# Pooled attention and a SiLU layer: selection matmuls in full 128-row shapes, and key transposition as a matmul with the identity

## The chip, the cores and the metric

The kernel runs on one core of a Trainium2 chip. The metric is the device time of one execution in microseconds, as the median of several runs. A core has engines that run side by side and wait for each other by semaphores: TensorE (PE; its weight loads are shown apart as PEld), VectorE (DVE), ScalarE (ACT), GpSimd (POOL) and SyncE (SP), the last two here mainly as issuers of transfers. A matmul takes a weight tile, of so many rows (the dimension summed over, laid out over SBUF partitions) by so many columns (the rows of the result), and moves columns of a second operand through it; the result goes to PSUM.

## The reference

Eight batches, eight heads, 576 positions, 64 elements per head. Keys and values are pooled over groups of eight positions, so each head has 72 pooled keys; then plain softmax attention, and a layer with SiLU on the result (4608 tokens, 512 to 2048 to 512).

```python
def _attn_ref(q, k, v):
    B, H, S, D = q.shape              # 8, 8, 576, 64
    pool = 8
    Sp = S // pool                    # 72
    scale = 1.0 / np.sqrt(D)
    k_p = k.reshape(B, H, Sp, pool, D).mean(axis=3)
    v_p = v.reshape(B, H, Sp, pool, D).mean(axis=3)
    scores = scale * np.matmul(q, k_p.transpose(0, 1, 3, 2))
    # ... softmax over the last axis ...
    return np.matmul(attn, v_p)

def _moe_ref(x, w_in, w_out):
    h = x @ w_in
    g = h * (1.0 / (1.0 + np.exp(-h)))
    return g @ w_out
```

## The kernel before

The kernel works on tiles of 512 tokens. While TensorE computes the layer of one tile (`up`, then `down`), the attention of the next batch is woven into its stream at fixed places. The layer's products are computed in part by a scheme with seven products of quarters instead of eight, which is where VectorE gets much of its work. The stream starts with products of zeros (`warm_up`) while the first data is on its way.

Pooling differs by batch. For batches 0 to 2, the 576 pooled rows of all heads (8 heads of 72) are laid out over 128 partitions in five slots: four slots of 128 rows and a last one of 64. A head of 72 rows therefore lies across slots. Matmuls with pieces of an identity matrix ("selection") bring each head's rows to their place: for the keys with the sums as weights, which also transposes them (32 weight columns at a time), for the values with a shifted identity as weights.

```python
shifts = singles.tile([128, SP + 128 + SP], BF16, name="shifts")   # SP = 72
ident = shifts[:, SP : SP + 128]           # zeros, identity, zeros
# ...
RE = POOL * D
ROWS = H * SP                              # 576
SLOTS = ROWS // 128                        # 4
REST = ROWS - 128 * SLOTS                  # 64
k5, v5 = (singles.tile([128, SLOTS + 1, D], BF16, name=f"{n}5") for n in "kv")
# ...
def segments(h):
    r = SP * h
    while r < SP * (h + 1):
        i = r // 128
        e = min(SP * (h + 1), 128 * (i + 1))
        yield i, (128 if i < SLOTS else REST), r - 128 * i, r - SP * h, e - r
        r = e

def select_k(b, a):
    st = batches[b]
    if a == 0:
        st["kz_ps"] = ps_tile([128, 2, 2, SP], FP32, "at", "kz_ps")
    for c in range(2):
        for s in range(4):
            for i, n, r, sp, m in segments(4 * a + s):
                nc.tensor.matmul(
                    st["kz_ps"][32 * s : 32 * (s + 1), a, c, sp : sp + m],
                    lhsT=k5[:n, i, c * DH : (c + 1) * DH],
                    rhs=ident[:n, r : r + m], start=True, stop=True,
                )
# ...
def select_v(b, a, tag="at"):
    # ...
    for h in range(4 * a, 4 * (a + 1)):
        segs = list(segments(h))
        for j, (i, n, r, sp, m) in enumerate(segs):
            x = SP + r - sp
            nc.tensor.matmul(
                st["v_ps"][:SP, h, :], lhsT=shifts[:n, x : x + SP], rhs=v5[:n, i],
                start=(j == 0), stop=(j == len(segs) - 1),
            )
```

Each of `select_k` and `select_v` is called twice per batch, for heads 0 to 3 and 4 to 7. Rows 64 to 127 of the last slot's inputs are set to zero once at the start, so the sums there are zero.

For batches 3 to 7 each head's 72 pooled rows lie on 72 partitions, and the keys are transposed by TensorE:

```python
def k_transpose(b, parts=(0, 1)):
    st = batches[b]
    kT_ps = ps_tile([128, 2, 2, SP], BF16, "at", "kT_ps")
    for a in parts:
        for c in range(2):
            nc.tensor.transpose(
                kT_ps[:, a, c, :],
                st["kp"][:, a, c].rearrange("k s d -> k (s d)"),
                ident[:SP, :SP],
            )
    a0, a1 = parts[0], parts[-1] + 1
    nc.scalar.copy(kz[b % 2][:, a0:a1], kT_ps[:, a0:a1])
```

The start of the stream, where batch 0 is worked on (cut):

```python
warm_up(19)
slot_sums("k", 0)
select_k(0, 0)
copy_k(0, 0, act_copy)
warm_up(4)
q_transpose(0, 0, 0)
scores(0, part(0, 0))
slot_sums("k", 1)
warm_up(3)
select_k(0, 1)
copy_k(0, 1, act_copy)
# ...
slot_sums("v", 1)
warm_up(1)
numerators(0, part(0, 0), ("mm", "at"))
warm_up(2)
select_v(0, 1, "mm")
copy_v(0, 1)
q_transpose(0, 1, 1)
# ...
```

Of the kernel before, what the change touches and what calls it, by code (L numbers as in the profile page):

```python
# [27 lines left out]
FP32 = mybir.dt.float32  # L28
FP32R = mybir.dt.float32r
BF16 = mybir.dt.bfloat16  # L30
# [6 lines left out]
def kernel(  # L37
# [9 lines left out]
    nc = tc.nc  # L47
# [3 lines left out]
    SP = S // POOL  # L51
# [17 lines left out]
    DH = D // 2  # L69
# [12 lines left out]
    singles = ctx.enter_context(tc.tile_pool(name="singles", bufs=1))  # L82
    big = ctx.enter_context(tc.tile_pool(name="big", bufs=1))
    mid = ctx.enter_context(tc.tile_pool(name="mid", bufs=2))
# [6 lines left out]
    def ps_tile(shape, dtype, tag, name):  # L91
        return psum.tile(shape, dtype, tag=tag, bufs=banks[tag], name=name)

    shifts = singles.tile([128, SP + 128 + SP], BF16, name="shifts")
    ident = shifts[:, SP : SP + 128]
    ones = singles.tile([SP, 32], BF16, name="ones")
    warm = singles.tile([128, 512], BF16, name="warm")
# [17 lines left out]


    kz = [singles.tile([128, 2, 2, SP], BF16, name=f"kz{n}") for n in range(2)]
    gate = singles.tile([128, 1], FP32, name="gate")  # L120

    batches = {}

# [63 lines left out]
    def add_halves(raw):  # L187
        nc.vector.tensor_add(
            out=raw[:, :, : 2 * D], in0=raw[:, :, : 2 * D], in1=raw[:, :, 2 * D :]
        )  # L190

    def add_rest(dst, raw):
        nc.vector.tensor_add(
            out=dst,
            in0=raw[:, :, :D].rearrange("k h (c d) -> k h c d", c=2),
            in1=raw[:, :, D : 2 * D].rearrange("k h (c d) -> k h c d", c=2),
        )

    def pool_k(b, stage):
        st = batches[b]  # L200
        raw = st["k_raw"]
        if stage == 0:
            add_halves(raw)
            return
        st["kp"] = mid.tile([SP, 2, 2, 4, DH], BF16, tag="kp", bufs=1, name="kp")
        for i in range(2):
            add_rest(
                st["kp"][:, i].rearrange("k c s d -> k s c d"), raw[:, 4 * i : 4 * (i + 1)]
            )

    def pool_v(b):
# [4 lines left out]

    def k_transpose(b, parts=(0, 1)):
        st = batches[b]
        kT_ps = ps_tile([128, 2, 2, SP], BF16, "at", "kT_ps")
        for a in parts:  # L220
            for c in range(2):
                nc.tensor.transpose(
                    kT_ps[:, a, c, :],
                    st["kp"][:, a, c].rearrange("k s d -> k (s d)"),
                    ident[:SP, :SP],
                )
        a0, a1 = parts[0], parts[-1] + 1
        nc.scalar.copy(kz[b % 2][:, a0:a1], kT_ps[:, a0:a1])
# [5 lines left out]
    SLOTS = ROWS // 128  # L234
    REST = ROWS - 128 * SLOTS
    k5, v5 = (singles.tile([128, SLOTS + 1, D], BF16, name=f"{n}5") for n in "kv")
# [44 lines left out]
    def segments(h):  # L281
        r = SP * h
        while r < SP * (h + 1):
            i = r // 128
            e = min(SP * (h + 1), 128 * (i + 1))
            yield i, (128 if i < SLOTS else REST), r - 128 * i, r - SP * h, e - r
            r = e

    def select_k(b, a):
        st = batches[b]  # L290
        if a == 0:
            st["kz_ps"] = ps_tile([128, 2, 2, SP], FP32, "at", "kz_ps")
        for c in range(2):
            for s in range(4):
                for i, n, r, sp, m in segments(4 * a + s):
                    nc.tensor.matmul(  # L296
                        st["kz_ps"][32 * s : 32 * (s + 1), a, c, sp : sp + m],
                        lhsT=k5[:n, i, c * DH : (c + 1) * DH],
                        rhs=ident[:n, r : r + m], start=True, stop=True,
                    )  # L300

    def copy_k(b, a, copy=nc.vector.tensor_copy):
# [2 lines left out]
# [3 lines that stand above are left out]
            st["v_ps"] = ps_tile([128, H, D], FP32, tag, "v_ps")  # L308
            st["vp"] = mid.tile([SP, H, D], BF16, tag="vp", name="vp")
        for h in range(4 * a, 4 * (a + 1)):  # L310
            segs = list(segments(h))
            for j, (i, n, r, sp, m) in enumerate(segs):
                x = SP + r - sp
                nc.tensor.matmul(
                    st["v_ps"][:SP, h, :], lhsT=shifts[:n, x : x + SP], rhs=v5[:n, i],
                    start=(j == 0), stop=(j == len(segs) - 1),
                )

# [397 lines left out]
    attn_tables()  # L716
    nc.vector.memset(warm, 0.0)
    nc.vector.memset(ones, float(POOL))
    nc.gpsimd.memset(shifts, 0.0)
    make_identity(nc, ident, nomemset=True)  # L720

# [17 lines left out]
# [11 lines that stand above are left out]
    q_transpose(0, 1, 0)  # L750
# [3 lines left out]
    slot_sums("v", 0)  # L754
    warm_up(2)
    select_v(0, 0, "mm")
    copy_v(0, 0, act_copy)
    denominators(0, part(1, 0))
# [4 lines left out]
# [5 lines that stand above are left out]
# [21 lines left out]
    for t in range(NT):  # L789
        a = t + 1  # L790
# [41 lines left out]
        if a < B:  # L832
            q_at = [15, 16, 17, 8] if t > 1 else [24, 25, 26, 2] if t else [82, 84, 86, 88]
            if t == 0:
                for j in range(2):
                    f_up.append((44 + 8 * j, lambda j=j: slot_sums("k", j)))
                    f_up.append((72 + 8 * j, lambda j=j: select_k(1, j)))
                    f_up.append((72 + 8 * j, lambda j=j: copy_k(1, j)))
                    f_down.append((20 + 10 * j, lambda j=j: slot_sums("v", j)))
                    f_down.append((37 + 3 * j, lambda j=j: select_v(1, j, "at")))  # L840
                    f_down.append((37 + 3 * j, lambda j=j: copy_v(1, j)))
            elif t == 1:
                for j in range(2):
                    f_up.append((0, lambda j=j: slot_sums("k", j, halves=True)))
                    f_up.append((22, lambda j=j: select_k(2, j)))
                    f_up.append((23, lambda j=j: copy_k(2, j)))
                    f_down.append((8, lambda j=j: slot_sums("v", j, halves=True)))
                    f_down.append((40, lambda j=j: select_v(2, j, "at")))
                    f_down.append((41, lambda j=j: copy_v(2, j)))
            else:  # L850
                f_up.append((22, lambda: k_transpose(a)))
                f_down.append((10, lambda: pool_v(a)))
# [3 lines left out]
            if t == 0:  # L856
                f_down.append((0, lambda: load_half_2("k", 0)))
                f_down.append((0, lambda: load_q(2)))
                f_down.append((0, lambda: load_half_2("k", 1)))
                for half in range(2):  # L860
                    f_down.append((31, lambda half=half: load_half_2("v", half)))
                for y in range(2):
                    for n in U_W:
                        f_down.append((6, lambda y=y, n=n: unit_weight_sum(y, n)))
            elif a + 1 < B:
                for stage in range(2):
                    f_down.append((100, lambda stage=stage: pool_k(a + 1, stage)))
                f_up.append((0, lambda: load_one(a + 1, "k")))
                f_up.append((48 if a + 1 == B - 1 else 1, lambda: load_q(a + 1)))
                f_up.append((2, lambda: load_rest(a + 1, "k")))  # L870
                f_down.append((11, lambda: load_one(a + 1, "v")))
                f_down.append((12, lambda: load_rest(a + 1, "v")))
# [49 lines left out]
```

The softmax here doesn't subtract the row's maximum and nothing guards it: scores larger than these inputs give would overflow.

## Time and profile before

| what | value |
|---|---|
| time, median of 3 runs | 286.77 us (286.44 to 287.31) |
| span of the profiled execution | 284.8 us |
| granted TensorE clock | full |
| key selections (line 296) | 72 matmuls: 66 of 128 rows, 6 of 64 rows, 32 weight columns |
| value selections (line 314) | 36 matmuls: 33 of 128 rows, 3 of 64 rows, 72 weight columns |
| key transpositions (line 222) | 20, of 72 rows, 128 weight columns |
| median length of one | 190, 199 and 195 ns |
| ScalarE copy after a transposition (line 228) | 5, of 417 ns |

In the profile's rows a matmul is written as line, tiles (out<-in), weight rows*columns, and rows x columns of the moving operand. Matmuls are pipelined and their ends are modelled, so lengths overlap; the distance from one start to the next tells more. A row's idle time stands in square brackets with what ended it.

### The profile page before, as it was taken

To read this page: it belongs to the slowest core of one execution; us is meant where nothing else is said; L and a number is where in the kernel's file an instruction comes from. 1 tells how busy PE (TensorE), PEld (TensorE's weight loads), DVE (VectorE), ACT (ScalarE), POOL (GpSimd) and SP (SyncE) were. 2 spreads that over 40 slices of the span, in tenths; PEclk is the share of its full clock that TensorE was granted. 3 is DMA by queue.
4 is the path that set the end of the run, shared out by engine and by line. 5 is a ranking of instruction groups with operands and counts; after the bars stand their busy time and mean duration, and the time that the engine had idled before them with its cause. 6 is when DMAs were issued, how large, how long until landed. Compare 5 with 4: busy or idle time off the path is not lost.

```text
span 284.8 us, 6920 instructions
## 1 busy us (share of the span) xinstructions
PE 278.0 (98%) x2773; PEld 196.0 (69%) x2793; DVE 225.1 (79%) x403; ACT 183.8 (65%) x359; POOL 52.2 (18%) x68
## 2 busy tenths in 40 slices
PE   8989999999999999999999999999999999999995
PEld 3348544465777677767888886677677867787684
DVE  4887854979969796979698969986998686836773
ACT  1577676458656886688568857794779558325700
POOL 8664317402030011101200101054100000000000
PEclk9999999999999999999999999999999999999999
DMA  7999999793849565964895396839970032005004
GB/s 211 277 266 227 219 306 183 214 199 70 153 69 210 124 96 95 145 148 126 140 177 156 72 147 113 176 59 170 150 142 0 2 85 65 2 9 139 1 3 147
DMA packets 35296, 37.70 MB, mean 132 GB/s; under 512 B 9952, under 2 KB 27616, under 8 KB 35264
## 3 DMA queue, kind: packets, MB, share of 16 engines
q0 software_dynamic: 21760, 20.86, 43.0%
q1 hardware_dynamic: 12928, 15.48, 22.2%
q10 hardware_dynamic: 576, 0.92, 0.9%
q8 instruction: 22, 0.36, 0.6%
q14 instruction: 10, 0.08, 0.1%
HBM read 36.70 MB, written 9.44 MB: 162 GB/s over the span
## 4 chain that ended last, share of the span: by engine, by line
PE 94%; DVE 3%; ACT 1%; issue 1%; DVEq 0%
PE hp_ps L547 25%; PE o_psP L655 15%; PE o_psQ L655 15%; PE u_psQ L488 7%; PE u_psP L488 7%; PE o_psR L655 5%; PE sc_ps L351 4%; PE warm_ps L704 4%; PE o_ps L582 3%; PE nu_ps L395 3%; PE u_psR L488 2%; PE den_ps L369 2%; DVE w_sum L633 1%; PE kz_ps L296 1%; DVE xT L404 1%
## 5 line engine op out<-in xcount | busy, mean ns | idle before, releaser
L547 PE MATMUL hp_ps<-xT,w_in_sb 128*128 128x512 bf16 (+3 forms) x397 | 80.8, 338 | 1.4 <-ACT h_T L553 0.4
L655 PEld LDWEIGHTS <-h_sum 128*128 128x128 bf16 x640 | 60.6, 98 | 11.9 <-issue 1.3
L553 ACT ACTIVATE h_T<-hp_ps 128x512 bf16<-128x512 f32 (+2 forms) x95 | 51.4, 546 | 26.3 <-PE hp_ps L547 24.9
L547 PEld LDWEIGHTS <-w_in_sb 128*128 128x128 bf16 x412 | 39.3, 98 | 25.0 <-issue 1.4
L615 DVE TENSOR_TENSOR h_sum<-h_T 128x1024 bf16<-128x1024 bf16 (+1 forms) x72 | 50.8, 743 | 7.0 <-ACT h_T L553 7.0
L359 ACT ACTIVATE es<-sc_ps 72x384 bf16<-72x384 f32 (+1 forms) x100 | 39.0, 470 | 10.0 <-PE sc_ps L351 9.9
L488 PEld LDWEIGHTS <-w_sum 128*128 128x128 bf16 x300 | 29.4, 98 | 7.7
L655 PEld LDWEIGHTS <-h_T 128*128 128x128 bf16 x256 | 24.1, 98 | 4.4 <-issue 0.9
L404 DVE TENSOR_TENSOR xT<-nu_ps,rec 128x384 bf16<-128x384 f32 (+1 forms) x50 | 24.0, 532 | 0.3
L378 ACT ACTIVATE lnd<-den_ps 128x384 f32<-128x384 f32 (+1 forms) x23 | 11.1, 484 | 20.2 <-PE den_ps L369 20.2
L153 DVE STREAM_TRANSPOSE qT<-q_bf 128x576 bf16<-128x576 bf16 x32 | 23.0, 753 | 0.0
L182 POOL DMA_DIRECT2D raw<-in_k_dram x5 | 7.0, 1398 | 79.2 <-DVE h_sum L615 28.8
L496 ACT ACTIVATE h_T<-c_sb 128x512 bf16<-128x512 f32 x30 | 18.1, 625 | 5.0 <-DVE c_sb L520 5.0
L274 DVE TENSOR_TENSOR raw<-raw 128x384 f32<-128x384 f32 (+3 forms) x20 | 12.4, 618 | 7.5 <-DMA raw<-in_v_dram 4.3
L655 PE MATMUL o_psP<-w_out_sb,h_sum 128*128 128x256 bf16 x128 | 17.6, 273 | 0.0
L655 PE MATMUL o_psQ<-w_sum,h_sum 128*128 128x256 bf16 x128 | 16.7, 273 | 0.0
L655 PE MATMUL o_psQ<-w_out_sb,h_sum 128*128 128x256 bf16 x128 | 16.6, 273 | 0.0
L655 PE MATMUL o_psQ<-w_sum,h_T 128*128 128x256 bf16 x128 | 16.5, 273 | 0.0
L655 PE MATMUL o_psP<-w_sum,h_T 128*128 128x256 bf16 x128 | 16.5, 273 | 0.0
L520 DVE TENSOR_TENSOR c_sb<-u_psP,t_sb 128x512 f32<-128x512 f32 x15 | 10.2, 678 | 7.1 <-PE u_psP L488 3.6
L655 PE MATMUL o_psR<-w_sum,h_sum 128*128 128x256 bf16 x128 | 15.7, 273 | 0.0
L655 PE MATMUL o_psP<-w_sum,h_sum 128*128 128x256 bf16 x128 | 15.4, 272 | 0.0
(77 smaller groups left out, 417.1 us busy)
## 6 DMA issues: line engine op xcount, KB each, us to landing
out_dram<-o_sb SPq DMA_DIRECT2D x128, 64.0 KB, 3.0
q_bf<-in_q_dram POOLq DMA_DIRECT2D x6, 576.0 KB, 11.1
raw<-in_k_dram SPq DMA_DIRECT2D x6, 512.0 KB, 5.0
raw<-in_k_dram POOLq DMA_DIRECT2D x5, 576.0 KB, 9.1
raw<-in_v_dram POOLq DMA_DIRECT2D x5, 576.0 KB, 8.6
raw<-in_v_dram SPq DMA_DIRECT2D x5, 512.0 KB, 7.6
w_in_sb<-in_moe_w_in_dram POOLq DMA_DIRECT2D x8, 256.0 KB, 8.4
w_out_sb<-in_moe_w_out_dram POOLq DMA_DIRECT2D x4, 512.0 KB, 13.5
```

Source lines behind the costliest of these rows:

```text
L153: nc.vector.transpose(out=st["qT"][:, a, f * QF : (f + 1) * QF].rearrange("r i c p -> r (i c p)"), in_=st["q_bf"][:, a, f * n : (f + 1) * n],)
L274: nc.vector.tensor_add(out=raw[..., :w], in0=raw[..., :w], in1=raw[..., w : 2 * w])
L351: nc.tensor.matmul(sc[s][:, cs], lhsT=kz[b % 2][rows, g, c, :], rhs=st["qT"][rows, g, i0:i1, c, :], start=(c == 0), stop=(c == 1),)
L359: nc.scalar.activation(es[:, s, :], sc[s], func=AF.Exp, scale=score_scale)
L404: nc.vector.tensor_mul(out=xT[:, 2 * g0 + c : 2 * (g0 + ng - 1) + c + 1 : 2, cols], in0=nu[c][:, :w].rearrange("r (g n) -> r g n", g=ng), ...
L488: nc.tensor.matmul(ps[bank][:, u, :], lhsT=w[:, kk, 128 * u : 128 * (u + 1)], rhs=x[:, kk, :], start=first and u == 0 and kk == 0, stop=kk ...
L496: nc.scalar.activation(h_T[:, g : g + 2, j * NQ : (j + 1) * NQ], src, func=AF.Silu)
L547: nc.tensor.matmul(hp_ps[:, r0:r1], lhsT=w_in_sb[:, kk, g * 128 : (g + 1) * 128], rhs=xT[:, kk, x0 : x0 + r1 - r0], start=(kk == 0), stop= ...
L553: nc.scalar.activation(h_T[:, g, n0 : n0 + n], hp_ps[:, :n], func=AF.Silu)
L615: nc.vector.tensor_tensor(out=h_sum[n][:, ks, :], in0=quarter(*a, ks), in1=quarter(*b, ks), op=op)
L655: nc.tensor.matmul(ps[b][:, c, :], lhsT=left(n, kt, c), rhs=W_OUT[n][:, kt, :], start=b not in begun, stop=kt == k1 - 1, skip_group_check= ...
L704: nc.tensor.matmul(warm_ps, lhsT=warm[:, :128], rhs=warm, start=True, stop=True)
```

## The change

All selection matmuls take 128 rows: the fifth slot is read whole, its upper 64 rows being zero. The value selections are 128 weight columns wide instead of 72 (the rows 72 to 127 of their result are not used); the tile with the identity gets 56 more zero columns for that. The transposition of the keys becomes an ordinary matmul with the identity, with 128 rows: the pooled keys move to a tile of their own with 128 rows, cleared once at the start, of which 72 are written. Its result in PSUM is fp32. The purpose is that these matmuls have the same shape of the array as the layer's matmuls around them.

```diff
-    shifts = singles.tile([128, SP + 128 + SP], BF16, name="shifts")
+    shifts = singles.tile([128, SP + 256], BF16, name="shifts")
@@
-    gate = singles.tile([128, 1], FP32, name="gate")
+    kp = singles.tile([128, 2, 2, 4, DH], BF16, name="kp")
@@ pool_k
-        st["kp"] = mid.tile([SP, 2, 2, 4, DH], BF16, tag="kp", bufs=1, name="kp")
         for i in range(2):
             add_rest(
-                st["kp"][:, i].rearrange("k c s d -> k s c d"), raw[:, 4 * i : 4 * (i + 1)]
+                kp[:SP, i].rearrange("k c s d -> k s c d"), raw[:, 4 * i : 4 * (i + 1)]
             )
@@ k_transpose
-        kT_ps = ps_tile([128, 2, 2, SP], BF16, "at", "kT_ps")
+        kT_ps = ps_tile([128, 2, 2, SP], FP32, "at", "kT_ps")
         for a in parts:
             for c in range(2):
-                nc.tensor.transpose(
+                nc.tensor.matmul(
                     kT_ps[:, a, c, :],
-                    st["kp"][:, a, c].rearrange("k s d -> k (s d)"),
-                    ident[:SP, :SP],
+                    lhsT=kp[:, a, c].rearrange("k s d -> k (s d)"),
+                    rhs=ident[:, :SP], start=True, stop=True,
                 )
@@ segments
-            yield i, (128 if i < SLOTS else REST), r - 128 * i, r - SP * h, e - r
+            yield i, r - 128 * i, r - SP * h, e - r
@@ select_k
-                        lhsT=k5[:n, i, c * DH : (c + 1) * DH],
-                        rhs=ident[:n, r : r + m], start=True, stop=True,
+                        lhsT=k5[:, i, c * DH : (c + 1) * DH],
+                        rhs=ident[:, r : r + m], start=True, stop=True,
@@ select_v
-                    st["v_ps"][:SP, h, :], lhsT=shifts[:n, x : x + SP], rhs=v5[:n, i],
+                    st["v_ps"][:, h, :], lhsT=shifts[:, x : x + 128], rhs=v5[:, i],
@@ start
+    nc.vector.memset(kp, 0.0)
```

More of the change, by code (lines that the diff above doesn't have):

```diff
@@ L294, in select_k @@
             for s in range(4):
-                for i, n, r, sp, m in segments(4 * a + s):
+                for i, r, sp, m in segments(4 * a + s):
                     nc.tensor.matmul(
                         st["kz_ps"][32 * s : 32 * (s + 1), a, c, sp : sp + m],
-                        lhsT=k5[:n, i, c * DH : (c + 1) * DH],
-                        rhs=ident[:n, r : r + m], start=True, stop=True,
+                        lhsT=k5[:, i, c * DH : (c + 1) * DH],
+                        rhs=ident[:, r : r + m], start=True, stop=True,
                     )
@@ L311, in select_v @@
             segs = list(segments(h))
-            for j, (i, n, r, sp, m) in enumerate(segs):
+            for j, (i, r, sp, m) in enumerate(segs):
                 x = SP + r - sp
                 nc.tensor.matmul(
-                    st["v_ps"][:SP, h, :], lhsT=shifts[:n, x : x + SP], rhs=v5[:n, i],
+                    st["v_ps"][:, h, :], lhsT=shifts[:, x : x + 128], rhs=v5[:, i],
                     start=(j == 0), stop=(j == len(segs) - 1),
```

## The prediction

> **What bounds the kernel now.** I read the page first: busy times, then the chain that ended last.
>
> ```profile
> PE 278.0 (98%) x2773; PEld 196.0 (69%) x2793; DVE 225.1 (79%) x403; ACT 183.8 (65%) x359; POOL 52.2 (18%) x68
> ...
> PE 94%; DVE 3%; ACT 1%; issue 1%; DVEq 0%
> ```
>
> TensorE is busy 278.0 of 284.8 us and makes up 94% of the chain that set the end. So TensorE time that goes away should shorten the run, except where TensorE would only wait for another engine. The table of TensorE's waits has six rows: 1.2 us at the start, and none of the others over 0.4 us in total. What counts is therefore not how long one of the changed matmuls is "busy" (their ends are modelled and overlap) but how much later the next matmul starts. For that I took the timeline of TensorE around each group that the change touches. The columns are start, length, engine, line, operation, tiles, weight rows*columns, moving operand, count.
>
> Key selection for batch 1, which falls inside the first up projection:
>
> ```profile
> 28.23 0.28 PE L296 MATMUL kz_ps<-shifts,k 128*32 128x72 bf16 x12
> 28.43 0.94 PE L547 MATMUL hp_ps<-xT,w_in_sb 128*128 128x224 bf16 x8
> 29.30 0.64 PE L296 MATMUL kz_ps<-shifts,k 128*32 128x72 bf16 x12
> 29.88 0.56 PE L547 MATMUL hp_ps<-xT,w_in_sb 128*128 128x224 bf16 x4
> ```
>
> Both groups have twelve matmuls over 576 columns in all. The first (heads 0 to 3) delays the projection by 28.43 - 28.23 = 0.20 us, the second (heads 4 to 7) by 29.88 - 29.30 = 0.58 us. What differs is that in the second, two of the twelve read slot 4, which has 64 rows. One by one, the starts there show a pause of about 0.1 us before and after each 64-row matmul, while its neighbours start 2 to 30 ns apart.
>
> Value selection for batches 1 and 2, from two windows of the same view:
>
> ```profile
> 45.31 0.37 PE L314 MATMUL v_ps<-v,shifts 128*72 128x64 bf16 x6
> 45.52 0.81 PE L582 MATMUL o_ps<-w_out_sb,h_T 128*128 128x512 bf16 x3
> 46.19 0.48 PE L314 MATMUL v_ps<-v,shifts 128*72 128x64 bf16 x6
> 46.60 0.60 PE L582 MATMUL o_ps<-w_out_sb,h_T 128*128 128x512 bf16 x2
> ```
>
> ```profile
> 73.99 0.69 PE L314 MATMUL v_ps<-v,shifts 128*72 128x64 bf16 x12
> 74.61 0.61 PE L655 MATMUL o_psR<-w_sum,h_sum 128*128 128x256 bf16 x4
> ```
>
> Six value selections of 128 rows take 0.21 us, 35 ns each; six of which the last has 64 rows take 0.41 us. Batch 2 has all twelve in one go: 0.62 us.
>
> Key transposition (batches 3 to 7), batch 3 shown:
>
> ```profile
> 89.13 0.38 PE L547 MATMUL hp_ps<-xT,w_in_sb 128*128 128x512 bf16 x1
> 89.35 0.29 PE L222 MATMUL kT_ps<-shifts,kp 72*128 72x72 bf16 x4
> 89.48 0.60 PE L547 MATMUL hp_ps<-xT,w_in_sb 128*128 128x512 bf16 x2
> ```
>
> Four transpositions of 72 rows take 0.13 us, 33 ns each, and there is no pause on either side: 89.35 - 89.13 = 0.22 us is the usual step of a 512-column matmul here. 72 rows cost nothing beside a 128-row neighbour; 64 rows do.
>
> **What the Trainium skill says.** "TensorEngine Tiling (Array Packing)", section Tiling Modes, says that changing the tiling mode (not just the tile) drains TensorE, and lists 64-row modes apart from 128-row ones. The trace agrees: about 0.1 us per change, and only around the 64-row matmuls and between 32-column and 128-column groups. "TensorE: Matmul & The Clock Gate", section Weight-path perf modes, says that fast weight load is on when there are 128 weights and the type is not FP32. The trace agrees in direction: a value-selection load of 72 columns takes 117 ns on average, a 128-column load for the transposition 97 ns. The same page, section LDWEIGHTS, says that the load time goes with the columns and not with the rows: 93 ns (128 rows) against 89 ns (64 rows) for 32 columns here, so filling rows with zeros should be nearly free. "Perfetto Trace Analysis", section Transposes, advises transpose over an ordinary matmul; nothing in this run shows what the matmul form costs.
>
> **The change, part by part.** The order of instructions on each engine, and what each waits for, stays the same; only one DVE memset is new.
>
> 1. *Key selection to 128 rows.* Twelve matmuls per batch half stay twelve, with the same columns. The second half should become like the first: 0.58 to 0.20, so 0.38 us per batch. In batch 2 both halves stand together, but its two 64-row matmuls have the same pauses, so 0.38 us again. Three batches (0, 1, 2): 1.14 us.
>
> 2. *Value selection to 128 rows and 128 weight columns.* The pauses go: 0.41 - 0.21 = 0.20 us per batch. The wider load should bring the step from 35 ns to that of the transpositions or a little less, as 64 columns move instead of 72: I take 30 ns, 12 x 5 = 0.06 us. Together 0.26 us per batch (batch 2: 0.62 to 0.36). Three batches: 0.78 us.
>
> 3. *Transposition as matmul.* Twenty matmuls, each still a 128-column load and 72 moving columns. 72 rows are not a mode of their own in the trace, so I expect 0. The ScalarE copy behind it now reads fp32 instead of bf16 out of PSUM; it has 288 elements per row and takes 417 ns now. ScalarE is 65% busy, and an fp32 copy of 144 elements takes 279 ns, in line with 417 for 288. Also 0.
>
> 4. *New work.* Clearing kp (128x512 bf16) is the size of the 0.27 us memset of warm; it stands on DVE before 2.93 us in which DVE waits for the first keys. The cleared shifts tile grows from 272 to 328 columns, 0.38 to about 0.46 us on GpSimd, done near 6.5 us and first used at 7.97 us. Both lie beside the path.
>
> On TensorE this sums to 1.14 + 0.78 = 1.92 us. Not all of it counts. In batch 0, before 20 us, the other engines pace the start. Timelines of ScalarE, then VectorE:
>
> ```profile
> 9.92 0.99 ACT L359 ACTIVATE es<-sc_ps 72x288 bf16<-72x288 f32 x3
> 10.95 0.28 ACT L303 CAST kz<-kz_ps 128x144 bf16<-128x144 f32 x1
> ```
>
> ```profile
> 13.48 1.15 DVE L274 TENSOR_TENSOR raw<-raw 128x512 f32<-128x512 f32 x2 [0.61 <-DMA raw<-in_v_dram]
> 14.66 0.29 DVE L278 TENSOR_TENSOR v<-raw 128x128 bf16<-128x128 f32 x1
> 14.87 0.81 DVE L404 TENSOR_TENSOR xT<-nu_ps,rec 128x288 bf16<-128x288 f32 x2
> 15.80 0.42 DVE L321 CAST vp<-v_ps 72x256 bf16<-72x256 f32 x1
> 16.15 0.76 DVE L153 STREAM_TRANSPOSE qT<-q_bf 128x576 bf16<-128x576 bf16 x1
> ```
>
> The second key copy on ScalarE starts at 10.95, and the exponentials before it end at 10.91: an earlier key selection finds ScalarE still busy. VectorE is busy from the landing of the values at 13.48 to 15.68, then waits 0.12 us for the value selection; TensorE in turn waits 0.26 us for the transposition at 16.15. So batch 0 gives at most what lets that copy start nearer 15.6: I count 0.2 us of the possible 0.64. Batches 1 and 2 I count in full: 0.64 each. Sum 0.2 + 0.64 + 0.64 = 1.48 us; 286.77 - 1.48 = 285.3 us.
>
> **The rivals.** *VectorE takes the gain of batch 1.* At 53.8 us the second projection matmul of the next tile starts 0.22 us late, just after the last xT product ends. If VectorE's work before it were paced by a transfer, the 0.64 us would be lost: 285.9 us. Against it: VectorE's last three waits before that stretch (2.74, 0.56 and 0.33 us, up to 47.46 us) all end with TensorE, so VectorE moves forward with it. *The pauses are not the 64 rows* but something that stays, such as the end of an accumulation group or the fifth slot arriving late: then nothing is gained, 286.8 us. For it: one matmul of the slot does wait for a semaphore. Against: the pauses come back in batches 1 and 2, where the slot had been ready for over a microsecond. *The matmul form of the transposition is slower.* If each of the five groups had a pause before and after, 5 x 0.2 = 1.0 us is lost: 286.3 us. Against: nothing in loads or columns changes. *Transfers.* In the built program the sums and raw tiles move by 32 bytes against multiples of 64; if the loads of keys and values landed later for that, the VectorE waits of 2.93, 0.27 and 0.61 us at the start would grow, by tenths. The weights already lie at such places and load without trouble. *More than predicted:* batch 0 in full adds 0.44, 284.8 us.
>
> **Range and chances.** The three runs before spread over 0.87 us, so a median may be off by 0.3. Gains from 0.4 (a rival takes most) to 2.1 us give 284.6 to 286.4. Two per cent are 5.7 us, three times everything the change touches on TensorE, so same is nearly certain.
>
> **What would show it.** Right: the second key group of batch 1 delays the projection by 0.20 to 0.22 us instead of 0.58, the twelve value selections of batch 2 by 0.34 to 0.40 instead of 0.62, the weight load at that line falls below 105 ns, the four transpositions stay at 0.13 us and the copy behind them at 417 ns. Wrong: pauses still around the slot of 64 rows; value selections at 35 ns or more; a pause at the transpositions; a longer wait of VectorE for the first loads; or batches 3 to 7, where nothing should change, differing in length by more than 0.1 us each.

## The result and the profile after

The change made no difference: 287.1 us against 286.93 us before (medians of six runs each; 286.12 to 287.16 and 286.44 to 287.33), ratio 0.9997 with a 95% interval of 0.998 to 1.0014. The prediction had 285.3 us and a range of 284.6 to 286.4, so the measured time lies above the range. And yet nearly every sign that the prediction named for being right is in the profile of the changed kernel. First its busy times and the chain that ended last:

```profile
PE 278.7 (98%) x2793; PEld 194.5 (68%) x2793; DVE 225.2 (79%) x404; ACT 183.7 (65%) x359; POOL 52.1 (18%) x68
...
PE 89%; DVE 5%; DMA 2%; ACT 1%; issue 1%; SPq 0%; DVEq 0%
```

TensorE is as busy as before, but its share of the chain fell from 94% to 89%, and transfers and VectorE came in. (Twenty more matmul records than before are no more work: some were missing in the first trace.) Next the timeline of TensorE at the key selection of batch 1; the changed lines now stand one line higher in the kernel:

```profile
28.13 0.28 PE L295 MATMUL kz_ps<-shifts,k 128*32 128x72 bf16 x12
28.34 0.94 PE L546 MATMUL hp_ps<-xT,w_in_sb 128*128 128x224 bf16 x8
29.21 0.29 PE L295 MATMUL kz_ps<-shifts,k 128*32 128x72 bf16 x12
29.44 0.27 PE L546 MATMUL hp_ps<-xT,w_in_sb 128*128 128x224 bf16 x1
```

The second half now delays the projection by 29.44 - 29.21 = 0.23 us, where it was 0.58. The same view at the value selections of batch 2, and at the transpositions of batch 3:

```profile
73.00 0.51 PE L313 MATMUL v_ps<-v,shifts 128*128 128x64 bf16 x12
73.35 0.49 PE L654 MATMUL o_psR<-w_sum,h_sum 128*128 128x256 bf16 x3
```

```profile
88.25 0.29 PE L221 MATMUL kT_ps<-shifts,kp 128*128 128x72 bf16 x4
88.38 0.60 PE L546 MATMUL hp_ps<-xT,w_in_sb 128*128 128x512 bf16 x2
```

Twelve value selections take 0.35 us instead of 0.62, four transpositions 0.13 us as before; the value selection's weight load takes 98 ns instead of 117, the ScalarE copy behind the transpositions 420 ns (417 before). So the time on TensorE is really saved. The group after the value selections of batch 2 starts at 73.35 us, and at 74.61 before: 1.26 us ahead with all selections done. Some 0.16 us go soon after, where a weight load waits 0.23 us for VectorE's copy of the pooled values (line 394, at 75.60 us), so that the transpositions of batch 3 are 1.10 us ahead (88.25 against 89.35). At the end nothing is left. Nearly all of it is lost at two places, both in the products of an up projection. The timeline of TensorE in tile 5:

```profile
173.07 0.60 PE L487 MATMUL u_psQ<-xT,w_sum 128*128 128x256 bf16 x4
174.15 0.61 PE L487 MATMUL u_psR<-x_sum,w_sum 128*128 128x256 bf16 x4 [0.48 <-DVE x_sum L454]
```

TensorE stands still for x_sum, which VectorE makes. The timeline of VectorE just before says why it is late:

```profile
169.33 1.02 DVE L403 TENSOR_TENSOR xT<-nu_ps,rec 128x384 bf16<-128x384 f32 x2
171.15 1.22 DVE L188 TENSOR_TENSOR raw<-raw 72x1024 f32<-72x1024 f32 x1 [0.80 <-DMA raw<-in_k_dram]
...
173.68 1.75 DVE L454 TENSOR_TENSOR x_sum<-xT 128x512 bf16<-128x512 bf16 x5
```

In this trace VectorE takes its instructions one behind the other. Line 188 is the first addition of the key pooling for a later batch (here batch 6); it stands ahead of the x_sum additions in VectorE's stream, and 0.80 us went by until its keys had landed. The keys of a batch come in two loads: SyncE's writes half of the positions into the raw tile, and GpSimd's, issued after that, adds the second half to them. In the kernel before, the same place read:

```profile
170.22 1.02 DVE L404 TENSOR_TENSOR xT<-nu_ps,rec 128x384 bf16<-128x384 f32 x2
171.26 1.22 DVE L188 TENSOR_TENSOR raw<-raw 72x1024 f32<-72x1024 f32 x1
```

No wait is marked there, but the room was already gone. The semaphore events of that trace put the landing at 171.23 us, and line 188 starts 1.04 us after the start of the xT products, where 0.94 us are enough when the keys are there early (169.05 to 169.99, further below): the keys held VectorE by about 0.1 us. In the changed kernel VectorE came 0.9 us earlier, and the keys landed at 171.12, hardly earlier than before. In tile 3 (batch 4) the wait is 0.23 us, and there the landing itself moved: 112.01 us, against 109.61 before. Over the whole execution of the changed kernel:

```profile
its engine sat idle before it (us, times) until:
  DMA raw<-in_k_dram: 1.0, 2
```

The key pooling waited for keys twice, 1.0 us in all. Of the 1.10 us that the changed kernel was ahead at batch 3, 0.1 us is left at 176 us.

### The profile page after: what moved, and what is told of

The parts are those of the page before. It is cut to its first block, busy times and chain, and to the rows that moved or that the text cites. A ratio compares the mean times of both kernels' runs of the same rounds, so it can differ in the third digit from the quotient of the medians.

```text
span 284.7 us, 6941 instructions
## 1 busy us (share of the span) xinstructions
PE 278.7 (98%) x2793; PEld 194.5 (68%) x2793; DVE 225.2 (79%) x404; ACT 183.7 (65%) x359; POOL 52.1 (18%) x68
## 3 DMA queue, kind: packets, MB, share of 16 engines
q0 software_dynamic: 21760, 20.86, 44.6%
q1 hardware_dynamic: 12928, 15.48, 22.8%
## 4 chain that ended last, share of the span: by engine, by line
PE 89%; DVE 5%; DMA 2%; ACT 1%; issue 1%; SPq 0%; DVEq 0%
PE hp_ps L546 25%; PE o_psP L654 15%; PE o_psQ L654 15%; PE u_psQ L487 7%; PE u_psP L487 7%; PE o_psR L654 5%; PE sc_ps L350 4%; PE o_ps L581 3%; PE nu_ps L394 3%; PE u_psR L487 2%; PE den_ps L368 2%; DMA raw<-in_k_dram 2%; DVE raw L273 1%; DVE w_sum L632 1%; DMA out_dram<-o_sb 1%; DVE xT L403 1%
## 5 line engine op out<-in xcount | busy, mean ns | idle before, releaser
L546 PE MATMUL hp_ps<-xT,w_in_sb 128*128 128x512 bf16 (+3 forms) x412 | 82.6, 340 | 0.5 <-ACT h_T L552 0.4
L581 PE MATMUL o_ps<-w_out_sb,h_T 128*128 128x512 bf16 x64 | 15.3, 380 | 0.0
```

The costliest lines, as they stand in the source:

```text
L546: nc.tensor.matmul(hp_ps[:, r0:r1], lhsT=w_in_sb[:, kk, g * 128 : (g + 1) * 128], rhs=xT[:, kk, x0 : x0 + r1 - r0], start=(kk == 0), stop= ...
L581: nc.tensor.matmul(ps, lhsT=h_T[:, g, m * 128 : (m + 1) * 128], rhs=w_out_sb[:, g, :], start=(g == 0), stop=(g == KG - 1),)
```

## The experiments

Two explanations stood against each other. **A:** the second half of the keys lands just when VectorE needs it, so whatever TensorE gains earlier is lost there. **B:** the change moved the raw tiles, and all that lie behind them in SBUF, from multiples of 64 bytes to 32 bytes past one (the four-byte tile it removed had taken 32 bytes, the tiles it added or widened 1152 more); that makes transfers slower, and the slower transfers ate the gain. (The first expectation below names batches 5 and 6; the pooling that waited was that of batches 4 and 6.) All ratios below are against the kernel before, with their 95% intervals.

### The place of the tiles

```diff
+    gate = singles.tile([128, 1], FP32, name="gate")   # in the changed kernel
-    gate = singles.tile([128, 1], FP32, name="gate")   # in the kernel before
```

The changed kernel with the unused tile put back:

> The changed kernel with one unused 32-byte tile put back, so that the sums and the raw tiles again start at multiples of 64 bytes. Theory A (the keys of batches 5 and 6 land just when VectorE needs them, and VectorE then holds up TensorE, so TensorE's gain is lost there whatever the placement): no difference, 286.5 to 287.2 us. Theory B (the placement 32 bytes past a multiple of 64 makes the loads slower, and that ate the gain): 285.3 to 285.9 us, and the loads of keys and values take as long from issue to landing as before (median 9.1 and 8.6 us).

Measured: 285.6 us (284.73 to 286.59), ratio 0.9959 (0.9945 to 0.9973). That is what B expected.

The kernel before without it:

> The kernel before without its unused 32-byte tile, so that the sums and the raw tiles start 32 bytes past a multiple of 64, as in the changed kernel. Theory A: no difference from before, 286.6 to 287.2 us. Theory B: slower by about what the changed kernel lost, 287.8 to 288.4 us.

Measured: 287.3 us, ratio 1.0013 (1.0001 to 1.0025): slower, but by about a third of what B expected, and 0.1 us above A's range. The transfers themselves differ as B says. The table of DMA queues has, for each, packets, megabytes and the share of the 16 engines' time that its packets took. The hardware queue (key and value first halves, outputs) in the kernel before, then in the kernel before without the tile:

```profile
q1 hardware_dynamic: 12928, 15.48, 22.2%
```

```profile
q1 hardware_dynamic: 12928, 15.48, 23.1%
```

In the changed kernel, then in the changed kernel with the tile put back:

```profile
q1 hardware_dynamic: 12928, 15.48, 22.8%
```

```profile
q1 hardware_dynamic: 12928, 15.48, 21.4%
```

The same bytes in the same packets take less of the engines' time wherever the raw tiles start at a multiple of 64. But the sign that goes with B alone is not there: of B's expectation that loads take as long as before, the software queue's keys fit (median 8.9 us) and the values do not (9.1 against 8.6). And the profiled execution of the changed kernel with the tile put back still loses about 0.9 us at x_sum in tile 3. So B is not the whole, and A is not refuted.

### Key pooling behind the sums

```diff
-                f_up.append((22, lambda: k_transpose(a)))
+                for stage in range(2):
+                    f_up.append((18, lambda stage=stage: pool_k(a, stage)))
+                f_up.append((40, lambda: k_transpose(a)))
@@
-                for stage in range(2):
-                    f_down.append((100, lambda stage=stage: pool_k(a + 1, stage)))
-                f_up.append((0, lambda: load_one(a + 1, "k")))
+                f_up.append((19, lambda: load_one(a + 1, "k")))
@@
-                f_up.append((2, lambda: load_rest(a + 1, "k")))
+                f_up.append((20, lambda: load_rest(a + 1, "k")))
```

In the changed kernel:

> The changed kernel with the pooling of the keys of batches 3 to 7 moved on VectorE from the end of one tile's down projection (ahead of the sums that the next tile's products need) into the next tile's up projection, behind those sums, the transposition later by 18 steps, and the next key load behind it. A late landing then holds up nothing on TensorE. Theory A: the lost gain comes back, 285.2 to 285.9 us, and TensorE's waits for ScalarE and VectorE at the second and third stage of the products of tiles 3 and 5 (1.1 us in the changed kernel's trace) go to under 0.2 us. Theory B: little changes if the loads are slow as such and other waits take over, 286.5 to 287.2 us.

In the kernel before:

> The kernel before with the same move of the key pooling. Theory A: it waits there for only 0.13 us in its profile, so at most a little is won, 286.3 to 287.0 us, and the difference to the changed kernel with the same move is the 1.3 to 1.5 us that TensorE saves. Theory B says nothing of it. If both moved kernels come out the same, the saved TensorE time is lost somewhere else than at the key pooling.

Measured: 290.47 us, ratio 1.0127 (1.0114 to 1.014), and 291.37 us, ratio 1.0162 (1.0149 to 1.0175). Both times lie more than 3 us above every expected range. The edit made a new wait at its new place. TensorE's waits in the second of the two kernels:

```profile
PE u_psQ L488 <- DVE rr_sb L508: 4.2, 5, 0.8
```

Five times, once in each of tiles 2 to 6, TensorE waits for a sum of the second unit's products, because the pooling (1.18 and 0.76 us) now stands ahead of it. VectorE's longest gap around it in tile 2 is 0.99 us, and the pooling takes 1.94. The two kernels stand 0.9 us apart, where A expected 1.3 to 1.5, but with the new wait in both the pair decides nothing between A and B; it does say that VectorE's order there is as tight as the keys' landing.

### Keys loaded earlier

The remaining way is to leave all engines' order alone and bring the keys sooner. SyncE issues the key load behind all sixteen output stores of a tile. Its timeline in the changed kernel:

```profile
140.24 13.80 SPq L566 DMA_DIRECT2D out_dram<-o_sb  x16
154.14 1.17 SPq L173 DMA_DIRECT2D raw<-in_k_dram  x2
```

The raw tile, however, is free as soon as the previous keys are pooled, between the first and the second eight stores. The edit:

```diff
-                f_up.append((0, lambda: load_one(a + 1, "k")))
+                if t == 1:
+                    f_up.append((0, lambda: load_one(a + 1, "k")))
+                if a + 2 < B:
+                    f_down.append((101, lambda: load_one(a + 2, "k")))
```

In the changed kernel, in the kernel before, and in the changed kernel with the tile put back:

> The changed kernel with the first-half key load of the next batch issued as soon as the raw tile is free, between the two groups of eight output stores of a tile instead of behind all sixteen; nothing else moves, and the order on TensorE, VectorE and ScalarE stays. The keys should then land some 6 us before VectorE needs them. Theory A (late keys hold up VectorE and so TensorE): 285.0 to 285.7 us, and none of the waits of 0.2 to 0.7 us that TensorE has at the second and third stage of the products in tiles 3 and 5. Theory B (the placement slows transfers and that costs time in other ways too): still near 286.5 to 287.

> The kernel before with the same earlier key load. Theory A: it loses little to late keys, so 286.2 to 286.9 us, and it stands 1.2 to 1.6 us above the changed kernel with the earlier load: the saving that TensorE's starts show. If the two come out within 0.5 us, the saving is lost elsewhere.

> Both: the changed kernel with the earlier key load and the 32-byte tile put back. If placement acts only through the late keys (A and B joined), it makes no further difference here: within 0.4 us of the kernel with the earlier load alone. If placement costs time by another way, it is 0.8 us or more faster.

Measured:

| kernel, keys earlier | us, median | ratio to the kernel before (95%) |
|---|---|---|
| changed | 285.04 | 0.9938 (0.9922 to 0.9954) |
| before | 286.42 | 0.9985 (0.9974 to 0.9996) |
| changed, tile put back | 284.98 | 0.9932 (0.9916 to 0.9948) |

SyncE's and then VectorE's timeline in the first of them:

```profile
139.96 7.49 SPq L566 DMA_DIRECT2D out_dram<-o_sb  x8
147.56 1.18 SPq L173 DMA_DIRECT2D raw<-in_k_dram  x2
148.86 6.65 SPq L566 DMA_DIRECT2D out_dram<-o_sb  x8
```

```profile
169.05 1.02 DVE L403 TENSOR_TENSOR xT<-nu_ps,rec 128x384 bf16<-128x384 f32 x2
169.99 1.21 DVE L188 TENSOR_TENSOR raw<-raw 72x1024 f32<-72x1024 f32 x1
```

The key load goes out 6.6 us earlier, the second half lands at 164.66 us, 5.3 us before it is needed, and line 188 follows the work before it without a wait. A is shown: with the keys out of the way the change is worth 286.42 - 285.04 = 1.38 us, where the prediction had 1.48. The third row joins B to it. The tile put back, worth 1.5 us between the medians (1.1 by the ratios) when keys are late, is worth nothing measurable when they are early, though the hardware queue's share again falls (22.9% to 20.5%). So slower transfers cost time here through the keys that VectorE waits for; a cost by another way, if there is one, is below what these intervals can show (some 0.6 us). And either remedy brings the changed kernel back into the predicted range: the tile put back with the keys still late (285.6 us), or the keys earlier with the tiles still 32 bytes off (285.04 us). The loss of the whole gain took both.

### Every tile at a multiple of 64 bytes

```diff
     ident = shifts[:, SP : SP + 128]
+    gap = singles.tile([128, 1], FP32, name="gap")     # changed kernel, keys earlier
     ones = singles.tile([SP, 32], BF16, name="ones")
```

> The changed kernel with the earlier key load and one unused 32-byte tile right behind the tile with the identity, which brings every large tile, those of the weights and of the outputs too, to a multiple of 64 bytes. If placement only acts through keys that land late: within 0.4 us of the two changed kernels with the earlier load (285.0 us), with a lower share of the DMA engines for the hardware queue (under 20.5%). If stores and weights matter at the end or the start, 0.4 us or more faster.

Measured: 284.96 us, ratio 0.9931 (0.991 to 0.9952), share of the hardware queue 20.1%. The weights' and outputs' places make no difference that can be measured.

### The parts of the change

All on the kernel before with the keys loaded earlier, tiles at multiples of 64 bytes. Only the transposition as matmul:

> The kernel before with the earlier key load, and of the change only the transposition as matmul with 128 rows (own tile for the pooled keys, cleared once, fp32 result). Tiles keep their places at multiples of 64 bytes. The step of the prediction (no gain, no loss): within 0.4 us of the kernel before with the earlier load (286.4 us). Rival (fp32 results or the matmul form cost a pause per group): 0.5 us or more slower.

Measured: 286.38 us, ratio 0.9979 (0.9969 to 0.9988), 0.04 us below the kernel it was built on. The transposition gives and costs nothing that can be measured.

Only the rows of the selections:

```diff
-            yield i, (128 if i < SLOTS else REST), r - 128 * i, r - SP * h, e - r
+            yield i, 128, r - 128 * i, r - SP * h, e - r
```

> The kernel before with the earlier key load, and of the change only the 128 rows of the selections; value selections stay 72 columns wide and the transposition stays. If the 64-row pauses are nearly the whole gain: 285.1 to 285.5 us, about 1.2 us below the kernel before with the earlier load. If the gain needs the 128 columns too, half of that or less.

Measured: 284.92 us, ratio 0.9922 (0.9901 to 0.9942), 0.2 us below the range expected for the first case. The whole gain is there.

Rows and width, without the transposition. The expectation on record describes the width alone; the kernel that ran under this name had both, so it is to be read against the two others:

> The kernel before with the earlier key load, and of the change only the selections: no 64-row shapes is left out of this one, only the value selections are made 128 columns wide and keep their rows, the last piece with 64 rows. The pauses around the 64-row matmuls stay, so if they are what costs time, the gain is no more than 0.3 us: 286.1 to 286.5 us. If the width is what matters, 285.0 to 285.4.

Measured: 284.9 us (284.8 to 285.0), ratio 0.9925 (0.9906 to 0.9943), the same as the rows alone. The width alone was then run by itself:

```diff
-    shifts = singles.tile([128, SP + 128 + SP], BF16, name="shifts")
+    shifts = singles.tile([128, SP + 256], BF16, name="shifts")
@@
-                    st["v_ps"][:SP, h, :], lhsT=shifts[:n, x : x + SP], rhs=v5[:n, i],
+                    st["v_ps"][:, h, :], lhsT=shifts[:n, x : x + 128], rhs=v5[:n, i],
```

> The kernel before with the earlier key load, and of the change only the width: value selections have 128 weight columns, and all pieces of the last slot keep their 64 rows. If the pauses around 64-row matmuls are the whole cost: within 0.4 us of the kernel before with the earlier load, 286.0 to 286.6 us, with about 0.1 us of pause still on each side of the 64-row pieces, and the value selections of 128 rows about 29 ns apart instead of 35. If the narrower weight load was what cost time: 285.0 to 285.5.

Measured: 286.06 us, ratio 0.9973 (0.996 to 0.9985). The value selections of batch 2 with the width alone, then with the rows alone:

```profile
73.53 0.62 PE L314 MATMUL v_ps<-v,shifts 128*128 128x64 bf16 x12
74.08 0.94 PE L655 MATMUL o_psR<-w_sum,h_sum 128*128 128x256 bf16 x7
```

```profile
72.60 0.58 PE L314 MATMUL v_ps<-v,shifts 128*72 128x64 bf16 x12
73.02 0.93 PE L655 MATMUL o_psR<-w_sum,h_sum 128*128 128x256 bf16 x7
```

From 0.62 us before, the width saves 0.07 and the rows 0.20; both together left 0.35. Three batches of 0.07 us are too little to be told apart in the time: the interval of the width alone overlaps that of the kernel it was built on.

## Why the prediction was wrong

By its own steps:

- *Key selection, 0.38 us per batch.* Right: 0.35 in batch 1 (0.58 to 0.23), and 0.35 in batch 2, where both halves take 0.33 us in the changed kernel (57.96 to 58.29 us) and 0.68 in the kernel before without its unused tile (58.90 to 59.58; in the kernel before itself a matmul record is missing there).
- *Value selection, 0.26 us per batch.* Right: 0.27 in batch 2 and 0.28 in batch 1 (0.62 to 0.34).
- *Transposition, 0.* Right, in the trace and by itself in the time. The advice of the Trainium skill ("Perfetto Trace Analysis", section Transposes) to use the transpose instruction rather than a matmul makes no difference at these sizes: 0.13 us for four either way.
- *Batch 0, at most 0.2 us of 0.64.* Too low by half, if anything. The second key selection of batch 0 starts at 10.27 us before and at 10.58 after, the first of batch 1 at 28.23 and 28.13: 0.41 us gained between them. The two executions did not start at the same pace, though, so part of this may be a wait that ran along.
- *"Batches 1 and 2 I count in full: 0.64 each."* This is the step that failed. TensorE did get ahead by what was counted, but in tiles 3 and 5 it waited for VectorE, which waited 0.23 and 0.80 us for keys, and then nothing was left. The prediction asked only whether another engine's next wait ends with TensorE, found that VectorE's did, and let everything behind it move along. What it did not ask is which transfers end just before they are needed. The view to ask was VectorE's timeline at line 188 with the landing beside it: in tiles 4 and 5 of the kernel before, the keys already landed last and held VectorE by about 0.1 us each (line 188 starts 1.07 and 1.04 us after the xT products instead of 0.94). This alone does not account for the whole loss, as the tile put back shows: with the keys still late, a ratio of 0.9959 was reached, about 1.2 us. The rest is the next point.
- *The rival "Transfers".* It named the right cause (tiles 32 bytes off) and looked for it at the wrong place, the first loads, where those waits did not grow, and "by tenths". It was set aside because "the weights already lie at such places and load without trouble". That was no evidence: none of TensorE's listed waits ended with a weight load, and whether the weights would load faster elsewhere was not shown. Here the placement was worth 1.1 to 1.5 us between the two changed kernels.
- *The rival that the pauses are not the 64 rows.* Refuted by the rows alone (0.9922) and by the pauses that are gone.
- *What would show it wrong.* One of its signs did: "batches 3 to 7, where nothing should change, differing in length by more than 0.1 us each". From the start of one tile's x_sum additions to the next, the step to tile 3 (batch 4) took 29.42 us against 29.10 before, and the step to tile 5 (batch 6) 30.01 against 29.20.

The mechanism of the saving was right, and by the medians its size within 0.1 us; the time was wrong because a second chain (stores, key load, second half of the keys, VectorE) runs beside TensorE's. In the kernel before it had no room in tiles 4 and 5, and in tile 3 its 3.2 us of room went when the keys landed 2.4 us later. TensorE alone busy for 98% of the time did not mean that TensorE alone sets the time.

Why the placement costs the kernel before only 0.13%, against 0.4% in the changed one, is argued and not shown: the kernel before arrives at the keys later, so a landing later by the same time delays it less. Single executions differ too in which tile waits: in the changed kernel tiles 3 and 5, with the tile put back tile 3 (keys at 112.34 us), in the kernel before without its tile tile 4, in the kernel before none by more than about 0.1 us.

## What to carry to other kernels

Before counting a saving in full, follow the loads that a tile further on needs: take the landing of each and the moment its reader is ready, and treat a load with little room as a second bound. Here a landing moved by 2.4 us from one kernel's profile to the other's, so even 3 us of room in one profile were not enough. If an instruction that waits for a load stands in an in-order stream ahead of work that the busiest engine needs, bring the load forward (here past eight stores in its queue) before speeding up the busiest engine. And when a change adds or removes small tiles, look where the large ones behind them come to lie.

## What the runs showed of the hardware

- A matmul with 64 rows among matmuls with 128 costs about 0.1 us before and after it; 72 rows cost nothing. Zeros in the missing rows cost next to nothing: the weight load took 93 ns with 128 rows and 89 with 64.
- A transposition by the transpose instruction (72 rows, bf16 out) and by a plain matmul with the identity (128 rows, fp32 out) took the same: 0.13 us for four. ScalarE's copy of 288 elements per row took 417 ns from bf16, and from fp32 417 ns in the kernel with the transposition alone and 420 in the changed one.
- Not expected: with the destinations 32 bytes past a multiple of 64, the same packets took more of the DMA engines' time, on the hardware queue 23.1% against 22.2%, 22.8% against 21.4%, 22.9% against 20.5%, and on the software queue 44.5% against 43.0%, 44.6% against 43.7%, 45.4% against 42.9%. Each pair is one profiled execution each way. Over all fourteen profiles of this case, the software queue took 44.5 to 45.7% in the four kernels 32 bytes off and 42.6 to 43.7% in the ten others; the hardware queue 22.8 to 23.5% and 20.1 to 22.7%, ranges that nearly touch. Plainest are the packets of 128 bytes: 46 to 53 ns on average 32 bytes off, 32 to 34 ns otherwise. Why is not shown.
